# Placing q/k transposes, last keys' transposes and the first gelus in a fused top-k attention and MLP kernel

## The chip, the cores and the metric

One core of a Trainium2 chip runs the whole kernel. The metric is the device time of one execution in microseconds (us); it is 1713.43 us for the kernel before (median of three runs, 1713.32 to 1719.77).

Five engines work side by side, each through its own queue of instructions in the order in which the program wrote them: PE (TensorE, matrix products and transposes), ACT (ScalarE, activations and copies out of PSUM), DVE (VectorE), POOL (GpSimd) and SP (SyncE, which here only issues transfers). PE's results land in PSUM, a small memory; a PSUM buffer can be written again only after some engine has copied it out.

## The reference

Attention in which every query keeps its 32 largest scores, followed by an MLP with an exact gelu. There are 8 batches, 8 heads, 576 tokens and a head size of 64; the MLP takes 4608 tokens of 512 channels through 2048 hidden ones.

```python
scores = scale * np.matmul(q, k.transpose(0, 1, 3, 2))
kth = np.partition(scores, -top_k, axis=-1)[..., -top_k:-top_k + 1]
scores = np.where(scores >= kth, scores, -1000000000.0)
attn = np.exp(scores - np.max(scores, axis=-1, keepdims=True))
attn = attn / (np.sum(attn, axis=-1, keepdims=True) + 1e-09)
attn_out = np.matmul(attn, v)
x = attn_out.transpose(0, 2, 1, 3).reshape(B * S, H * D)
h = x @ w_in
g = 0.5 * h * (1.0 + erf(h * inv_sqrt2))
out = g @ w_out
```

## The kernel before

**Items and slots.** Two heads form a pair; a batch has four. An item is a tile of 128 queries of both heads of a pair. A batch has 18 items: 16 of full tiles, and two in which the last 64 queries of two pairs share a tile. Even batches have those two last, odd batches first, so the order repeats every two batches, 36 items. One loop (line 609) runs over slots n, and every slot works on several items at once:

- `scores(n + 2)`: on PE a product for the last 64 keys (`t_ps`, line 290, or 304 for the shared tiles) and one for the other 512 (`s_ps`, 294 or 315); two scaling copies on ACT. I call it S.
- `attend(n - 3)`: for every second item the product of attention and values (`o`, line 458, or 468), and an ACT copy into `xT` (463). I call it O, or the product. When the last pair of a row of tiles is through, `n_tok` grows: 256 more tokens have all four pairs' channels.
- `softmax(n - 1, e)` for both heads: a Prelu (380) and an Exp (381) on ACT, which also sums (`den`).
- `transposes(n - 2)`: three groups. First the tails, that is the last 64 keys (`tp_t`, 409 or 414), then the 512 others of each head (`tp`, 427; M below), four transposes each. Each group ends in an ACT copy to `pt` or `ptt` (410, 419, 434).
- `top_k(n)` on DVE: eight MAX8 and six MATCH_REPLACE8. The reciprocal `rden` of item n - 1 (367) stands behind its last MAX8.
- `threshold(n)` and `normalise(n - 1)` on POOL (356, 359, 392). The transposes of an item need its normalised rows.

**q and k.** Before a pair's scores can start, its q and k blocks are transposed: ten PE transposes (line 249) in three groups of 4, 2 and 4, each with one ACT copy to `qk` (253). The first group holds four key blocks, the second the tails of q and k, the third the four query blocks. `prep_at` names one slot for each pair, and all three groups fall into it: the first behind the first half of the softmax, the others behind the last M groups.

**The MLP** is cut into 1152 pieces in a fixed order (`pieces`): a block of eight first-layer pieces (`h_ps`, line 506), then a block of eight second-layer pieces (`y_ps`, 542) of the block before, and so on. As the trace counts them, most first-layer pieces are four matmuls over 256 columns of xT, a second-layer piece two over 512 columns. `behind(work, x, us)` puts the gelus of two units (517, ACT) directly behind piece x. A first-layer piece may be placed only when `ready` has reached its tokens; `mlp(n)` places up to n pieces, `left` being what the slot may still take, 7 or 8. The first layer's PSUM tag "l1" and the second layer's "l2" have two buffers each. Gelu and Exp need different tables: where ACT goes from one to the other, an ACT_TABLE_LOAD of 1.28 us shows.

**The weights** come in as 16 units in slots 1 to 16: two or three ACT operations (183, 184, 188), one or two on POOL (199, 202) and one on DVE (210) for each. They stop after slot 16.

**PSUM.** `t_ps`, `o`, `tp_t`, `tp` and `tp_qk` share one tag, "tp", with two buffers that are taken in turn. So each of these groups has to wait until the group two places before it has been copied out by ACT; and ACT takes its copies in the order in which the loop wrote them, between the softmax and the gelus.

The order within a slot is that of the loop body below. `late` says whether the second half of the softmax stands behind the first M group or ahead of the transposes.

Of the kernel before, what the change touches and what calls it, by code (L numbers as in the profile page):

```python
# [14 lines left out]
def kernel(  # L15
# [20 lines left out]
    f32, i32, u32 = mybir.dt.float32, mybir.dt.int32, mybir.dt.uint32  # L36
# [4 lines left out]
    B, H, S, D = q.shape  # L41
    P = 128
# [3 lines left out]
    NP = H // 2  # L46
    NM = S // P
    SM = NM * P
# [12 lines left out]
    work = ctx.enter_context(tc.tile_pool(name="work", bufs=2))  # L61
# [19 lines left out]
    n_pairs = B * NP  # L81
    sources = {"q": q, "k": k, "v": v}

    def raw_of(n, pair):
        return raws[n][pair % len(raws[n])]

    def load(n, pair, queue=None):
        if pair >= n_pairs:
            return
        queue = queue or nc.sync  # L90
        b, h0 = pair // NP, 2 * (pair % NP)
        t, src = raw_of(n, pair), sources[n]
        for e in range(2):
            queue.dma_start(
                out=t[:, 0:NM, e, :], in_=src[b, h0 + e, 0:SM].rearrange("(t p) d -> p t d", p=P)
            )
            queue.dma_start(out=t[e * TL : (e + 1) * TL, NM, e, :], in_=src[b, h0 + e, SM:S])
# [23 lines left out]
    START = 2 * NP + 2  # L121
# [4 lines left out]
    def unit_in(n):  # L126
        return ORDER[n - FIRST] if 0 <= n - FIRST < UNITS else None
# [66 lines left out]
    def weights_add(u):  # L194
        if u in words:
            w, _, dst = parts(u)
            d = dst.bitcast(i32)
            if on_pool(u):
                nc.gpsimd.tensor_scalar(
                    w.bitcast(i32), w.bitcast(u32), 2.0**-13, None, op0=ALU.mult  # L200
                )
            nc.gpsimd.tensor_tensor(d, d, w.bitcast(i32), op=ALU.add)
# [14 lines left out]
    items, starts = [], []  # L217
# [17 lines left out]
    KT = SM + 2 * P  # L235
    qk_of = {}

    def transpose_qk(pair, first=False):

        t = work.tile([P, KT + SM], f32, tag="qk", bufs=NP + 2, name="qk")  # L240
        qk_of[pair] = t
        rq, rk = raw_of("q", pair), raw_of("k", pair)
        blocks = [(rq, j) for j in range(NJ)] + [(rk, NM)] + [(rk, j) for j in range(NM)]

        def piece(c, n):
            tp = ps.tile([P, 512], f32, tag="tp", name="tp_qk")
            for x in range(n):
                r, j = blocks[c + x]
                nc.tensor.transpose(  # L249
                    tp[:, x * P : (x + 1) * P], r[:, j].rearrange("p e d -> p (e d)"), ident  # L250
                )
            copy = nc.vector.tensor_copy if first and c > 0 else nc.scalar.copy
            copy(out=t[:, c * P : (c + n) * P], in_=tp[:, 0 : n * P])  # L253
            if c == 0:
                load("q", pair + 2)
                load("k", pair + 2)

        return [lambda c=c, n=n: piece(c, n) for c, n in ((6, 4), (4, 2), (0, 4))]
# [17 lines left out]
    def halves(t, e, step):  # L276

        return spread(t[:, e * TL :], step + (TL if e == 0 else -TL), TL)
# [84 lines left out]
    def inverse(i):  # L363
        if i < 0 or i >= N:
            return
        st = stat_of[i]
        nc.vector.reciprocal(st["rden"], st["den"])  # L367

    def add_small(i):
        if i < 0 or i >= N:  # L370
            return
        st = stat_of[i]
        nc.gpsimd.tensor_scalar(st["den"], st["den"], 1e-9, None, op0=ALU.add)  # L373

    def softmax(i, e):

        if i < 0 or i >= N:
            return
        st, s = stat_of[i], row(i, e)
        nc.scalar.activation(s, s, func=AF.Prelu, bias=st["neg"][:, e, 1:2], scale=1.0, alpha=STEEP)  # L380
        nc.scalar.activation(  # L381
            s, s, func=AF.Exp, bias=st["bias"][:, e : e + 1], scale=1.0,
            accum_out=st["den"][:, e : e + 1],
        )
# [13 lines left out]
    def transposes(i):  # L398

        if i < 0 or i >= N:  # L400
            return []
        t, s = items[i][1], S_of.pop(i)

        def tails():
            tp = ps.tile([P, 512], f32, tag="tp", name="tp_t")
            if t < NM:
                if t % 2 == 0:
                    pt_now[0] = work.tile([P, 2 * NM + 1, 2 * P], f32, tag="pt", name="pt")
                nc.tensor.transpose(tp[:, 0:P], s[:, SM : S + TL], ident)  # L409
                nc.scalar.copy(out=pt_now[0][:, 2 * NM, t % 2 * P : (t % 2 + 1) * P], in_=tp[:, 0:P])  # L410
            else:
                pt_now[0] = ptt
                for r in range(2):
                    nc.tensor.transpose(
                        tp[0:TL, r * P : (r + 1) * P], s[:, r * S + SM : (r + 1) * S], ident
                    )
                for e in range(2):
                    c = slice(e * TL, (e + 1) * TL)
                    nc.scalar.copy(
                        out=halves(ptt[c, 0, NM, :], e, NJ * P), in_=halves(tp[0:TL, 0 : 2 * P], e, P)  # L420
                    )

        def main(e):
            tp = ps.tile([P, 512], f32, tag="tp", name="tp")
            first = e * (S + TL if t < NM else S)
            for j in range(NM):
                nc.tensor.transpose(  # L427
                    tp[:, j * P : (j + 1) * P], s[:, first + j * P : first + (j + 1) * P], ident
                )
            if t < NM:  # L430
                dst = pt_now[0][:, e * NM : (e + 1) * NM, t % 2 * P : (t % 2 + 1) * P]
            else:
                dst = ptt[:, e, 0:NM, :]
            nc.scalar.copy(out=dst, in_=tp.rearrange("p (j n) -> p j n", j=NM))  # L434

        return [tails] + [lambda e=e: main(e) for e in range(2)]

    n_tok, read = [0], [0]
# [74 lines left out]
    def gelus(us):  # L513
        for u in us:
            _, n, _, nf = units[u]
            g_of[u] = work.tile([P, nf, n], f32, tag="g", bufs=4, name="g")
            nc.scalar.activation(g_of[u], h_of.pop(u), func=AF.Gelu)  # L517
# [37 lines left out]
    pieces = []  # L555
    GELU_AT = 5

    def block(u, first):

        do, need = (l1_piece, units[u][0] + units[u][1]) if first else (l2_piece, 0)  # L560
        return [(need, lambda w=w, x=x: do(w, x)) for w in (u, u + 1) for x in range(4)]

    def behind(work, x, us):
        need, f = work[x]
        work[x] = need, lambda: (f(), gelus(us))
        return work

    pieces += block(0, True) + behind(block(2, True), 0, (0, 1))
    for u in range(2, NU, 2):
        pieces += behind(block(u - 2, False), GELU_AT, (u, u + 1))  # L570
        if u + 2 < NU:
# [2 lines left out]
    done = [0]  # L574

    def mlp(n):
        for _ in range(n):
            if done[0] >= len(pieces) or pieces[done[0]][0] > ready[0] or left[0] == 0:
                return
            pieces[done[0]][1]()  # L580
            done[0] += 1
            left[0] -= 1


    ready, left = [0], [0]
# [13 lines left out]
            scores(0)  # L599
            scores(1)  # L600

    prep_at = {}
    for b in range(B):

        for p, at in enumerate((-6, -3, 0, 2) if b % 2 == 0 else (-6, -4, -3, -2)):
            if b or p > 1:
                prep_at[starts[b] + at] = b * NP + p
    ahead = N + 4
    for n in range(ahead):

        left[0] = 7 if n < START + 2 * NP else 8
        weights_add(unit_in(n))
        scores(n + 2)
        product = attend(n - 3)
        late = n > START
        mlp(1)
        prep = transpose_qk(prep_at[n]) if n in prep_at else []
        softmax(n - 1, 0)
        for piece in prep[0:1]:
            piece()  # L620
        mlp(1)
        if not late:
            softmax(n - 1, 1)
        mlp(1)
        tr = transposes(n - 2)
        for piece in tr[:2]:
            piece()
            ready[0] = n_tok[0]
            mlp(1)
        ready[0] = n_tok[0]  # L630
        if late:
            softmax(n - 1, 1)
        add_small(n - 1)
        for piece in tr[2:] + prep[1:]:
            piece()
            mlp(1)
        mlp(left[0])
        if n < N:
            top_k(n, {3: lambda: inverse(n - 1)})
        else:  # L640
            inverse(n - 1)
        threshold(n)
        normalise(n - 1)

        weights_sign(unit_in(n))
        weights_size(unit_in(n + 1))
        if n >= FIRST:
            load_weights(n + 2)
        if n <= NP:
            load("v", n)  # L650
# [36 lines left out]
```

## Time and profile before

| | |
|---|---|
| median time | 1713.43 us |
| span of the profiled execution | 1713.1 us |
| L506 first layer on PE | 559.3 us, 2560 matmuls |
| L542 second layer on PE | 546.1 us, 1152 matmuls |
| L341 and L344, top-k on DVE | 612.5 + 202.4 and 425.4 + 212.4 us |
| L380 and L381, softmax on ACT | 223.8 and 223.3 us |
| L392, normalise on POOL | 493.6 us |
| L427, M groups on PE | 179.6 us, 1152 transposes |

A span is cut in the page into 40 slices of 43 us, with the busy share of each engine in tenths. A row of waits says which engine stood at which line, for which engine and line it waited, how long in total, how often, and the longest. A wait for a buffer is shown with the copy that freed it as the releaser. PEld is PE's loading of the stationary operand, which runs beside the matmuls where nothing holds it. Slots are not marked in the trace. I find them by the first `t_ps` after a pause: slot 30 begins at 354.61 us, slot 46 at 534.98, slot 138 at 1564.40. The last slots end near 1640 us, and PE then works through the 56 pieces that are left.

### The profile page before, as it was taken

The numbers are of one execution on the slowest core, as the hardware profiler recorded it, in microseconds if no ns is written. First come the engines' busy times: TensorE is split into PE (matmuls) and PEld (weight loads), VectorE is DVE, ScalarE is ACT, GpSimd is POOL, SyncE is SP. The second block draws the span as 40 slices with busy tenths as digits, with TensorE's granted clock in tenths as the row PEclk, the third lists the DMA queues.
The fourth block names the chain that finished last, engine by engine and source line by source line (L and its number), as shares of the span: only waits on it lengthen the run. The fifth ranks groups of instructions, "written<-read, shape, count | busy, mean of one in ns | idle before, by whom it ended". The sixth has DMA issues, their size and how long they took to land.

```text
span 1713.1 us, 24404 instructions
## 1 busy us (share of the span) xinstructions
PE 1612.4 (94%) x8480; PEld 1093.2 (64%) x8480; DVE 1428.2 (83%) x3042; ACT 1189.2 (69%) x2147; POOL 663.0 (39%) x764
## 2 busy tenths in 40 slices
PE   5558999999999999999999999999999999999999
PEld 3336567766666667666666667676666666766665
DVE  6998989988799887998889888898889987899900
ACT  5877876767676767776767776776777776777730
POOL 3667833333233332333333323333333333333310
PEclk8669999999999999999999999999999999999999
DMA  5422210011100111002100011001110010000000
GB/s 157 133 99 87 84 48 1 13 27 24 40 13 1 41 29 41 1 13 49 28 27 1 27 42 41 1 14 27 29 48 1 13 29 15 21 1 13 7 13 13
DMA packets 126715, 56.10 MB, mean 33 GB/s; under 512 B 117888, under 2 KB 117888, under 8 KB 126592
## 3 DMA queue, kind: packets, MB, share of 16 engines
q1 hardware_dynamic: 125056, 52.16, 11.4%
q0 software_dynamic: 320, 2.10, 0.3%
q8 instruction: 67, 1.10, 0.3%
q14 instruction: 56, 0.46, 0.1%
q10 hardware_dynamic: 1216, 0.30, 0.1%
HBM read 45.08 MB, written 9.44 MB: 32 GB/s over the span
## 4 chain that ended last, share of the span: by engine, by line
PE 83%; ACT 6%; POOL 0%; issue 0%; ACTq 0%; POOLq 0%
PE h_ps L506 27%; PE y_ps L542 27%; PE o L458 8%; PE s_ps L294 7%; PE tp L427 6%; PE o L468 2%; PE t_ps L290 1%; PE tp_qk L249 1%; ACT s L381 1%; ACT L381 1%; ACT s L380 1%; PE s_ps L315 1%; PE tp_t L409 1%; ACT L517 1%; ACT g L517 1%; ACT pt L434 0%
## 5 line engine op out<-in xcount | busy, mean ns | idle before, releaser
L341 DVE MAX8 top<-rest 128x8 f32<-128x576 f32 x864 | 612.5, 754 | 0.0
L506 PE MATMUL h_ps<-xT,w_in_sb 128*128 128x256 f32 (+1 forms) x2560 | 559.3, 363 | 4.3 <-ACT g L517 4.3
L542 PE MATMUL y_ps<-w_out_sb,g 128*128 128x512 f32 x1152 | 546.1, 598 | 0.0
L392 POOL TENSOR_SCALAR s<-s,rden 128x576 f32<-128x576 f32 x288 | 493.6, 1723 | 0.8 <-issue 0.4
L506 PEld LDWEIGHTS h_ps<-xT,w_in_sb 128*128 128x128 f32 x2560 | 430.3, 192 | 66.6 <-issue 15.8
L344 DVE MATCH_REPLACE8 rest<-top,rest 128x576 f32<-128x576 f32 x576 | 425.4, 750 | 0.0
L373 POOL TENSOR_SCALAR den<-den 128x2 f32<-128x2 f32 x144 | 32.0, 222 | 884.0 <-ACT s L381 883.4
L542 PEld LDWEIGHTS y_ps<-w_out_sb,g 128*128 128x128 f32 x1152 | 196.2, 190 | 173.2 <-issue 172.7
L298 ACT ACTIVATE s<-s_ps 128x1024 f32<-128x1024 f32 x128 | 131.6, 1028 | 189.7 <-PE s_ps L294 189.7
L381 ACT ACTIVATE s<-s,bias 128x576 f32<-128x576 f32 x288 | 223.3, 775 | 12.8
L380 ACT ACTIVATE s<-s,neg 128x576 f32<-128x576 f32 x288 | 223.8, 777 | 1.6 <-POOL neg L356 1.1
L434 ACT COPY pt<-tp 128x512 f32<-128x512 f32 x256 | 147.3, 576 | 109.2 <-PE tp L427 108.5
L427 PEld LDWEIGHTS tp<-ident,s 128*128 128x128 f32 x1152 | 147.0, 145 | 118.5 <-issue 57.6
L344 DVE MATCH_REPLACE8 rest<-top,s 128x576 f32<-128x576 f32 x288 | 212.4, 748 | 0.0
L341 DVE MAX8 top<-s 128x8 f32<-128x576 f32 x288 | 202.4, 747 | 5.1 <-ACT s L299 5.1
L427 PE MATMUL tp<-ident,s 128*128 128x128 f32 x1152 | 179.6, 281 | 28.3 <-ACT qk L253 13.7
L367 DVE RECIPROCAL rden<-den 128x2 f32<-128x2 f32 x144 | 23.7, 164 | 194.2 <-POOL den L373 194.2
L294 PE MATMUL s_ps<-qk 64*128 64x256 f32 x1024 | 154.5, 423 | 3.5 <-ACT s L298 3.5
L458 PE MATMUL o<-pt,raw_v 128*64 128x256 f32 x1280 | 153.6, 387 | 2.1 <-ACT pt L434 2.1
L458 PEld LDWEIGHTS o<-pt,raw_v 128*64 128x64 f32 x1280 | 86.8, 138 | 66.9 <-issue 17.9
L294 PEld LDWEIGHTS s_ps<-qk 64*128 64x128 f32 x1024 | 92.9, 196 | 27.1 <-ACT s L298 4.0
L517 ACT ACTIVATE g<-h_ps 128x512 f32<-128x512 f32 x144 | 78.6, 595 | 37.8 <-PE h_ps L506 37.1
(65 smaller groups left out, 1106.6 us busy)
## 6 DMA issues: line engine op xcount, KB each, us to landing
raw_q<-in_q_dram SPq DMA_DIRECT2D x64, 128.0 KB, 2.3
raw_v<-in_v_dram SPq DMA_DIRECT2D x64, 128.0 KB, 2.4
out_dram<-y SPq DMA_DIRECT2D x32, 256.0 KB, 2.2
raw_k<-in_k_dram SPq DMA_DIRECT2D x62, 128.0 KB, 2.4
w_out_sb<-in_moe_w_in_dram SPq DMA_DIRECT2D x12, 511.8 KB, 4.7
w_out_sb<-in_moe_w_out_dram SPq DMA_DIRECT2D x10, 511.8 KB, 4.0
w_out_sb<-in_moe_w_in_dram POOLq DMA_DIRECT2D x4, 511.8 KB, 8.6
words<-in_moe_w_out_dram SPq DMA_DIRECT2D x4, 511.8 KB, 5.0
```

The source lines that it names most:

```text
L294: nc.tensor.matmul(s_ps[:, e, c * 256 : (c + 1) * 256], lhsT=lhsT[rows, :], rhs=qk[rows, KT + c * 256 : KT + (c + 1) * 256], start=True, s ...
L298: nc.scalar.activation(spread(s, S + TL, SM), s_ps, func=AF.Copy, scale=scale)
L341: nc.vector.max(st["top"][:, e, 8 * r : 8 * r + 8], cur[e])
L344: nc.vector.match_replace(rest[:, e], st["top"][:, e, 8 * r : 8 * r + 8], cur[e], LOWEST)
L380: nc.scalar.activation(s, s, func=AF.Prelu, bias=st["neg"][:, e, 1:2], scale=1.0, alpha=STEEP)
L381: nc.scalar.activation(s, s, func=AF.Exp, bias=st["bias"][:, e : e + 1], scale=1.0, accum_out=st["den"][:, e : e + 1],)
L392: nc.gpsimd.tensor_scalar(s, s, st["rden"][:, e : e + 1], None, op0=ALU.mult)
L427: nc.tensor.transpose(tp[:, j * P : (j + 1) * P], s[:, first + j * P : first + (j + 1) * P], ident)
L434: nc.scalar.copy(out=dst, in_=tp.rearrange("p (j n) -> p j n", j=NM))
L458: nc.tensor.matmul(o[e * D : (e + 1) * D, 0:n], lhsT=vt[:, j, e, :], rhs=pt[:, e * NM + j if j < NM else 2 * NM, :], start=(j == 0), stop= ...
L506: nc.tensor.matmul(h_tile(u)[:, i, :], lhsT=w_in_sb[:, ko, f * P : (f + 1) * P], rhs=xT[:, ko, c0 : c0 + n], start=(ko == 0), stop=(ko == ...
L542: nc.tensor.matmul(y_of[sub], lhsT=g_of[u][:, i, sub * P : (sub + 1) * P], rhs=w_out_sb[:, f, :], start=(f == 0), stop=(f == FT - 1),)
```

## The change

Three things move; no arithmetic is added or removed.

1. q and k: instead of all three groups in one slot, one group a slot, behind the slot's own last transposes. A table by batch parity and pair says which slots (`slots_of`, with `first` for pairs 2 and 3). The `qk` tile is taken when the first group is placed.
2. Last keys: in slots where a product has been placed and the next MLP piece needs its tokens, the tails' transposes come directly behind the product, ahead of the softmax, and `ready` is raised then. MLP pieces can so be placed from the slot's first half on.
3. First gelus: they move from behind the first piece of the second block to behind the last piece of the first block, and slot 10 may take 8 pieces instead of 7, so that this last piece falls in slot 10. `late` begins one slot later.

```diff
     def transpose_qk(pair, first=False):
-        t = work.tile([P, KT + SM], f32, tag="qk", bufs=NP + 2, name="qk")
-        qk_of[pair] = t
         ...
         def piece(c, n):
+            if pair not in qk_of:
+                qk_of[pair] = work.tile([P, KT + SM], f32, tag="qk", bufs=NP + 2, name="qk")
+            t = qk_of[pair]
             ...
-    pieces += block(0, True) + behind(block(2, True), 0, (0, 1))
+    pieces += behind(block(0, True), 7, (0, 1)) + block(2, True)
     ...
-        for p, at in enumerate((-6, -3, 0, 2) if b % 2 == 0 else (-6, -4, -3, -2)):
-            if b or p > 1:
-                prep_at[starts[b] + at] = b * NP + p
+    slots_of = [
+        [(-8, -7, -6), (-5, -4, -3), (-2, -1, 0), (1, 2, 3)],
+        [(-10, -9, -8), (-7, -6, -5), (-4, -4, -3), (-3, -2, -2)],
+    ]
+    first = {2: (0, 1, 1), 3: (2, 2, 3)}
+    prep_in = {}
+    for pair in range(2, n_pairs):
+        b, p = divmod(pair, NP)
+        for at, piece in zip(first.get(pair, slots_of[b % 2][p]), transpose_qk(pair)):
+            prep_in.setdefault(starts[b] + at, []).append(piece)
     ...
-        left[0] = 7 if n < START + 2 * NP else 8
+        left[0] = 7 if START < n < START + 2 * NP else 8
         weights_add(unit_in(n))
         scores(n + 2)
         product = attend(n - 3)
-        late = n > START
+        late = n > START + 1
         mlp(1)
-        prep = transpose_qk(prep_at[n]) if n in prep_at else []
+        tr = transposes(n - 2)
+        if product and done[0] < len(pieces) and pieces[done[0]][0] > ready[0]:
+            for piece in tr[:1]:
+                piece()
+            tr, ready[0] = tr[1:], n_tok[0]
         softmax(n - 1, 0)
-        for piece in prep[0:1]:
-            piece()
         mlp(1)
         if not late:
             softmax(n - 1, 1)
         mlp(1)
-        tr = transposes(n - 2)
-        for piece in tr[:2]:
+        for piece in tr[:-1]:
             piece()
             ready[0] = n_tok[0]
             mlp(1)
         ...
-        for piece in tr[2:] + prep[1:]:
+        for piece in tr[-1:] + prep_in.pop(n, []):
             piece()
             mlp(1)
```

More of the change, by code (lines that the diff above doesn't have):

```diff
@@ L600 @@
             scores(1)
-    prep_at = {}
-    for b in range(B):
-        for p, at in enumerate((-6, -3, 0, 2) if b % 2 == 0 else (-6, -4, -3, -2)):
-            if b or p > 1:
-                prep_at[starts[b] + at] = b * NP + p
+    slots_of = [
[8 more added lines that the diff above has]
+            prep_in.setdefault(starts[b] + at, []).append(piece)
     ahead = N + 4
     for n in range(ahead):
-        left[0] = 7 if n < START + 2 * NP else 8
+        left[0] = 7 if START < n < START + 2 * NP else 8
         weights_add(unit_in(n))
```

## The prediction

> **What bounds the kernel now.** I first read the busy shares and the slices.
>
> ```profile
> PE 1612.4 (94%) x8480; PEld 1093.2 (64%) x8480; DVE 1428.2 (83%) x3042; ACT 1189.2 (69%) x2147; POOL 663.0 (39%) x764
> PE   5558999999999999999999999999999999999999
> DVE  6998989988799887998889888898889987899900
> PEclk8669999999999999999999999999999999999999
> ```
>
> Two stages. Up to about 150 us DVE is full and PE is half idle at a low clock; from the fifth slice on PE is at 9. There the time is the length of PE's queue: its work plus its waits. So I asked for PE's waits between 240 and 1640 us, and DVE's between 40 and 240.
>
> ```profile
> PE tp L427 <- ACT qk L253: 12.8, 6, 2.1
> PE tp L427 <- ACT pt L410: 4.5, 4, 1.1
> PE tp L427 <- ACT ptt L419: 3.9, 3, 1.3
> PE t_ps L304 <- ACT qk L253: 2.5, 3, 0.8
> PE t_ps L290 <- ACT qk L253: 2.5, 3, 0.8
> DVE rden L367 <- POOL den L373: 14.1, 5, 8.3
> ```
>
> The first five are all of PE's waits there: 26.2 us, every one for an ACT copy that has not freed a "tp" buffer. They are few and regular, so I cut the trace at the first t_ps of each slot (columns: stretch, length, busy time of PE, PEld, DVE, ACT, POOL, clock, DMA).
>
> ```profile
> 354.61:369.86 15.25, 13.12 (x82) 10.16 (x81) 13.30 (x30) 9.83 (x19) 7.21 (x7) 1.00 0.05 11
> 390.89:402.34 11.45, 10.60 (x46) 5.63 (x45) 11.45 (x26) 8.71 (x17) 5.66 (x7) 1.00 0.05 12
> 414.13:423.47 9.34, 9.34 (x36) 4.87 (x35) 9.34 (x22) 6.61 (x12) 3.56 (x6) 1.00 0.01 2
> 423.47:436.26 12.79, 12.79 (x83) 10.21 (x81) 10.82 (x24) 9.83 (x19) 5.21 (x6) 1.00 0.10 23
> 471.89:483.58 11.69, 11.69 (x72) 9.26 (x71) 9.82 (x22) 9.35 (x18) 4.07 (x6) 1.00 0.13 46
> 534.98:547.97 12.99, 11.86 (x73) 9.17 (x72) 12.30 (x27) 8.38 (x16) 6.69 (x7) 1.00 0.01 1
> 626.17:639.41 13.24, 11.94 (x74) 9.27 (x73) 11.84 (x27) 8.73 (x17) 6.09 (x7) 1.00 0.01 1
> 849.98:865.26 15.28, 13.15 (x82) 10.16 (x81) 13.07 (x30) 9.82 (x19) 6.84 (x7) 1.00 0.18 40
> 1161.69:1564.40 402.71, 394.32 (x2121) 268.32 (x2120) 352.11 (x757) 288.74 (x530) 145.90 (x181) 1.00 0.08 21
> ```
>
> In order these are slots 30, 33, 35, 36, 40, 46, 54, 74 and the period of slots 102 to 137. A plain odd slot is 9.34 us and a plain even one, with its product, 11.69: PE full in both. Slot 36 adds ten q/k transposes in three groups and no wait: 12.79 - 11.69 = 1.10 us, 0.11 a transpose, so a group of four is 0.43 of stream. A slot above these sums holds waits.
>
> **What the Trainium skill says.** "PSUM — Partial Sum Buffer", Engine vs sequencer instructions: ScalarE's queue is strict FIFO and matmuls start in program order. The trace agrees: in slot 46 a tails copy whose transposes ended by 539.0 comes out at 542.0, behind a Prelu, a table load and an Exp, and PE stands 1.13 us. "Perfetto Trace Analysis", Optimization Strategy: a gap that repeats on the engine that should be full can mean too few buffers; here these are the two of tag "tp". "ScalarE: Activation LUTs", What ACT_TABLE_LOAD costs: about 1283 ns for the load and 1380 for a drain. The trace has 1.28 for the load (353.59 to 354.87) and no drain (the gelu starts at 354.88); I use 1.28.
>
> **Part 1: tails directly behind the product.** Where the next MLP piece needs the product (slots 4, 6, 8, 10, then 18, 30, 38, 46, 54 and their repeats, from my walk through the loop), PE now has S, O, tails, piece, piece, M instead of S, O, (q/k,) tails, piece, M, piece, M. ACT gets the tails copy ahead of the first softmax half instead of behind it. No instruction is added. In slot 46's clock: the product ends and tails start at 538.66, xT's copy is 538.81 to 539.18, the tails copy would follow to about 539.5. The first piece reads channels 0 to 255, which older copies filled, so it runs at once (before, too, at 538.83); the second, at about 539.7, finds xT copied. The first M takes the buffer that xT's copy freed, the second the one that the tails copy freed. So no wait is left. Behind the tails copy on ACT stands the softmax, 0.4 us later than now; den, rden and top_k wait for it, and in this slot DVE already waits 0.69 us. DVE's own work is 9.8 us a slot (9.82 in the row of slot 40) against a mean of 10.5 on PE, which hides it.
> Gain by slot, against 11.69 (and 1.08 of stream where ten transposes are in it): slot 30 15.25 - 12.77 = 2.48; slot 38, read at slot 74, 2.51; slot 46 1.30; slot 54 1.55. Part of the first two belongs to moving the q/k group that stands ahead of the tails.
>
> **Part 2: q/k groups one a slot, last in the slot.** The same ten transposes a pair, 1.08 us of stream, now in slots -8 to +3 around a batch. Gone: slot 33's wait, 11.45 - 9.34 - 1.08 = 1.03. Slot 51 keeps its wait (two groups behind a gelu). So the gain per period of 36 slots is 2.48 + 2.51 + 1.30 + 1.55 + 1.03 = 8.9; three periods 26.6, and slot 138 another 1.3: **27.9 us**.
> Two new waits. In odd slots the group stands behind the gelus on ACT. By the clock of slots 43 and 44 the gelus end at 515.30, so a four-block copy (0.58) runs to 515.8, and the next product, which takes that buffer and stood at 515.33, now 0.43 later at 515.76. I have no row of that pair. Bounds: 0, as above, and 0.58, the whole copy. I take 0.15, for a release and a weight load that cannot run ahead: eight such slots a period (29, 31, 33, 35, 37, 45, 47, 49), three periods: +3.6. Second, in slot 39 (third slot of an even batch) the last group of the fourth pair ends behind the gelus, and slot 40's t_ps reads it at once: PE is there at 513.95 + 0.43 = 514.4, the copy is done at 515.8. That is 1.46, at most 2.0 with a restart; I take 1.5, three times: +4.5. In even slots no gelu is ahead and the copy is out before the next use: nothing.
>
> **Part 3: first gelus in slot 10.** Before, slot 11 has them behind its first piece, the pieces of the next unit stand 3.81 us for the buffers (141.19), ACT's second softmax half comes last (to 150.84), and DVE stands from 142.9 to 151.18, the 8.3 above. After: slot 10 has one piece more (0.86) and a group (0.43), so its last h ends near 134.9 + 1.3 = 136.2; gelu out at 136.9; the two weight operations 2.3 (131.24 to 133.56 before), scores copies 1.3, Prelu, table load and Exp 3.0, second half 1.8 lead to 145.3, rden at 145.9. DVE waits 3.0: 5.3 less. PE in slot 11 stands for its last M until the tails copy at 145.6 and ends the slot near 148.4, not 150.2: 1.8 less. In slots 12 to 17 ACT is the tight one (58.45 of 69.51 us) and has three gelu pairs before and after, but q/k copies for 26 instead of 40 transposes: 4.0 against 6.1 us. Slot 18 comes between 1.8 + 2.1 = 3.9 and 5.3 + 2.1 = 7.4 earlier; I take **5**, since both engines feed it. That a slot-10 softmax now stands behind tails which wait for POOL costs nothing by the same sum: in slots 4 to 9 two slots of ACT's queue are about 21 us, DVE's 21.8 (top_k 9.65, sign 1.36), little room.
> The 56 pieces behind the last slot and their PE time stay.
>
> Sum: 1713.4 - 27.9 + 3.6 + 4.5 - 5 = 1688.6.
>
> **The rivals.**
> - Waits change place. If each group behind a gelu costs a whole copy (24 times 0.58 = 13.9), slot 40 costs 2.0 (6.0) and the start brings nothing: 1713.4 - 27.9 + 19.9 = 1705. For it: buffers stay two, and 2.5 us of waits behind the same gelus are in the trace. Against: they come where t_ps, not the later product, takes the buffer.
> - All of it lands: no wait behind gelus, 9 us at the start (the whole 8.3 and more): 1713.4 - 27.9 + 4.5 - 9 = 1681. The sum of ACT's queue in slot 11 speaks against.
> - Slower. The softmax behind the tails copy empties DVE: 3.9 us of softmax in each of slots 4, 6, 8 and 10 is 15.6, and every group behind a gelu holds t_ps as in slot 40, 24 times 1.46 = 35: 1713.4 + 15.6 + 35 + 4.5 - 27.9 - 5 = 1736. For it: ACT's 21 against 21.8. Against: t_ps takes another buffer in all but that slot.
>
> **How the numbers follow.** Chances: my sum 0.65, all of it 0.15, waits in other places 0.14, slower 0.06. Range 1678 to 1704: the low end a little under the second case, the high end nearly at the first, which stands just short of 0.5% (1704.9). Faster 0.86, same 0.08, slower 0.06. The clock matters too: "TensorE: Matmul & The Clock Gate", What's actually happening, says that an idle window halves it, and the trace has 0.50 in the idle stretches before 150 us; how often that happens at the start may move the time by 2 us or so either way.
>
> **What would show it.** The waits of tp on the tails copies and on qk gone from 240 to 1640 us; slots 46 and 54 at 12.1 and 11.7, slot 30 at 12.1; a new wait of t_ps on qk of about 1.5 us, three times, and small ones of o; DVE's longest wait near 3 us instead of 8.3; slot 18 near 215. Wrong if PE's waits keep their 26 us under other names, or if DVE waits again and again for rden after 240 us.

## The result, and the profile after

The changed kernel takes 1691.75 us (median of five runs, 1689.41 to 1693.2), the kernel before 1714.55 beside it. The ratio is 0.986, 95% interval 0.9841 to 0.9879. The sum of the prediction, 1688.6, is off by about 3 us. The two parts of that sum are not as good: the periods gained 2.5 us more than forecast, and the start, where 5 us were forecast, gained nothing. One execution further down (1715.7 us, of the kernel with the weight load first, at a mean clock of 0.953 where the others had 0.978 to 0.985) is left out of the comparisons as a slow one.

The page of the kernel after: the busy row, and the slices of PE, DVE and PE's clock.

```profile
PE 1611.4 (95%) x8480; PEld 1093.3 (65%) x8480; DVE 1428.8 (85%) x3042; ACT 1188.1 (70%) x2147; POOL 662.5 (39%) x764
...
PE   5659899999999999999999999999999999999999
...
DVE  6999798998889888998889888898889988899900
...
PEclk8669999999999999999999999999999999999999
```

The work is the same (PE 1611.4 us busy against 1612.4), the span is 23 us shorter. So waits went. These are all of PE's waits between 240 and 1640 us:

```profile
PE t_ps L291 <- ACT qk L254: 3.8, 3, 1.3
PE t_ps L305 <- ACT qk L254: 2.5, 3, 0.8
```

and this is DVE's one group of waits between 40 and 240 us:

```profile
DVE rden L368 <- POOL den L374: 13.9, 7, 7.9
```

PE's 26.2 us have become 6.3. No wait for the tails' copy is left; the three of 1.3 us are new and are those that the prediction put at slot 40; the three of 0.8 us are those of slot 51, which it left standing. DVE's row has hardly moved, 13.9 against 14.1 us, with a longest wait of 7.9 us where 3 was forecast.

The prediction also named a sign of being wrong: that DVE waits again and again for rden after 240 us. It does, but it did so before, and more. DVE's waits between 240 and 1640 us, before and after:

```profile
DVE rden L367 <- POOL den L373: 180.1, 93, 8.7
DVE rden L368 <- POOL den L374: 155.6, 87, 8.7
```

In slots 30, 46 and 54 below PE is full while DVE is not, so waits of DVE cost nothing there; as a sign they don't tell the two cases apart.

By slots (columns as before: stretch, length, busy time of PE, PEld, DVE, ACT, POOL, clock, DMA):

```profile
169.53:189.12 19.59, 14.68 (x73) 8.83 (x72) 11.74 (x23) 8.83 (x16) 10.90 (x8) 0.83 0.44 138
356.16:368.31 12.15, 12.15 (x76) 9.65 (x75) 10.84 (x26) 8.93 (x18) 5.08 (x7) 1.00 0.10 22
390.07:399.85 9.78, 9.78 (x40) 5.26 (x39) 9.78 (x24) 7.04 (x13) 3.99 (x6) 1.00 0.05 11
455.52:466.74 11.22, 9.95 (x41) 5.08 (x39) 10.66 (x25) 8.49 (x16) 4.91 (x7) 1.00 0.11 25
530.58:542.74 12.16, 12.16 (x77) 9.66 (x76) 10.84 (x26) 8.92 (x18) 5.14 (x7) 1.00 0.10 22
619.90:631.62 11.72, 11.72 (x73) 9.34 (x72) 10.26 (x24) 8.80 (x17) 4.51 (x6) 1.00 0.01 1
1147.57:1542.62 395.05, 392.92 (x2116) 268.13 (x2115) 351.66 (x757) 288.00 (x529) 145.31 (x181) 1.00 0.08 21
```

These are slots 14, 30, 33, 39, 46, 54 and the period of slots 102 to 137. Slots 30 and 46 are an even slot and one group of four (11.69 + 0.43 = 12.12), slot 54 a bare even slot, slot 33 an odd slot and a group (9.34 + 0.43 = 9.77): PE is full in all of them. Slot 39 has 1.45 us over 9.77, as the next slot's first product waits for its copy. Slot 14 is new: 19.59 us, with every engine well under its length and PE's clock down to 0.83.

Two figures carry the rest of the story. I read them at the first `s_ps` matmul of a slot: when slot 19 begins (the **start**: everything in which other engines than PE have a say), and the time from there to slot 141 (the **periods**).

| kernel | slot 19 begins, us | slots 19 to 141, us |
|---|---|---|
| before | 235.3 | 1363.4 |
| after | 236.2 | 1339.4 |

In the periods 24.0 us went. 1.7 us of them are a stretch of 3.4 us at half clock at 454 us in the trace of before (slot 38 took 16.96 us, its repeat 15.28). It comes directly behind one of the 2.1 us stands that the change removes:

```profile
453.24 0.66 PE L427 MATMUL tp<-ident,s 128*128 128x128 f32 x4 [2.12 <-ACT qk L253]
```

The forecast read slot 38 at its repeat and has no such stretch, so 22.3 us are to be held against it. The start lost 0.9 us.

How far can one trace be trusted on the start? Seven of the kernels here, the changed one and six of the experiments, are the same program up to slot 10, and DVE is full there. Yet the reciprocal that DVE runs in slot 10 comes at 131.1 us in one of these traces and at 132.7 us in another. So up to 1.6 us of a difference in the start can come from the execution and not from an edit. Where that matters I also count from this reciprocal to slot 19, which leaves that part out: 103.5 us before and 103.5 after.

### The profile page after: what moved, and what is told of

The parts are those of the page before. It is cut to its first block, busy times and chain, and to the rows that moved or that the text cites. A ratio compares the mean times of both kernels' runs of the same rounds, so it can differ in the third digit from the quotient of the medians.

```text
span 1690.0 us, 24403 instructions
## 1 busy us (share of the span) xinstructions
PE 1611.4 (95%) x8480; PEld 1093.3 (65%) x8480; DVE 1428.8 (85%) x3042; ACT 1188.1 (70%) x2147; POOL 662.5 (39%) x764
## 4 chain that ended last, share of the span: by engine, by line
PE 87%; ACT 5%; DVE 5%; POOL 1%; issue 1%; DMA 1%; SPq 0%; ACTq 0%; POOLq 0%
PE h_ps L507 29%; PE y_ps L543 28%; PE o L459 8%; PE s_ps L295 7%; PE tp L428 7%; DVE top L342 2%; PE o L469 2%; DVE rest L345 2%; PE tp_qk L250 2%; PE t_ps L291 2%; ACT s L382 1%; PE tp_t L410 1%; PE s_ps L316 1%; ACT s L381 1%; ACT L518 1%
```

## The experiments

The first question was where the 5 us of the start went. The trace shows slot 14 standing. From the timeline of the kernel after (start, duration; SPq is SyncE issuing transfers):

```profile
168.76 0.38 SPq L94 DMA_DIRECT2D raw_q<-in_q_dram  x1
...
172.75 0.51 SPq L97 DMA_DIRECT2D raw_k<-in_k_dram  x1
...
173.37 1.26 SPq L161 DMA_DIRECT2D xT<-in_moe_w_out_dram  x2
...
177.60 0.37 ACT L464 COPY xT<-o 128x256 f32<-128x256 f32 x1 [4.54 <-DMA xT<-in_moe_w_out_dram]
...
178.84 0.79 PE L507 MATMUL h_ps<-xT,w_in_sb 128*128 128x256 f32 x1 [4.91 <-DMA xT<-in_moe_w_out_dram]
```

The raw weights of unit 14 are staged in the last 512 columns of `xT` (line 159). In slot 14 the product's copy and the first layer both touch `xT`, and both wait for that transfer. It stands on SP's queue behind eight q/k loads, which the third q/k group of slot 13 issues: from 168.76 to 173.26, 4.5 us. That group is the sixth pair's (pair 5, counted from 0). Before, it stood in slot 14, and its loads came behind the weight load. From there the wait runs on: the copy is ahead of the softmax on ACT, DVE then stands 7.85 us for rden, and PE drops to half clock at 177.8 us for 6.8 us.

**Leaving out one part each.** Three kernels, each the changed one without one of its parts, and one with the q/k loads of slot 13 behind the weight load.

Without the tails order:

```diff
-        if product and done[0] < len(pieces) and pieces[done[0]][0] > ready[0]:
+        if False:
```

> The changed kernel with the last keys' transposes back behind the softmax half in every slot; q/k table and first gelus as changed. Theory, the parts add up slot by slot: slots 30, 38, 46 of each period get back the 1.3 us wait of slot 46 before and slot 54 its 1.55, three periods, and slot 138 another 1.3, so 3 x 5.45 + 1.3 = 17.7 us: about 1709 against 1691.75; PE waits for tp on the tails copy, 13 times. Rival, the tails order matters only where a q/k group stands ahead of the tails: at most 5 us, under 1697.

Measured 1709.1 us; ratio to before 0.9966 (0.9951 to 0.9981). PE's waits between 240 and 1640 us in that kernel:

```profile
PE tp L428 <- ACT pt L411: 11.2, 10, 1.1
PE tp L428 <- ACT ptt L420: 3.9, 3, 1.3
```

Thirteen waits for the tails' copy are back, ten plus three, besides the 6.3 us of the kernel after. The periods take 1357.2 us, 17.8 more than after. The first theory stands: the tails order is worth its wait in every slot where it applies.

Without the q/k table:

```diff
-        for at, piece in zip(first.get(pair, slots_of[b % 2][p]), transpose_qk(pair)):
-            prep_in.setdefault(starts[b] + at, []).append(piece)
         ...
+                prep_at[starts[b] + at] = b * NP + p
         ...
+        prep = transpose_qk(prep_at[n]) if n in prep_at else []
         softmax(n - 1, 0)
+        for piece in prep[0:1]:
+            piece()
         ...
-        for piece in tr[-1:] + prep_in.pop(n, []):
+        for piece in tr[-1:] + prep[1:]:
```

> The changed kernel with all three q/k groups of a pair back in one slot, in the places of before; tails order and first gelus as changed. Theory A (slot 14 of the changed kernel stands because the weight load into xT queues on SP behind the eight q/k loads that the group of slot 13 issues): here these loads are issued a slot earlier, slot 14 has no wait for a transfer and the start gains its 5 us, while the periods lose about 1 us of waits in slots 30, 33 and 38 each and get back 1.45 in slot 40: 1688 to 1692. Theory B (slots 12 to 17 are held by ACT's own queue, the wait for the transfer only takes the place of others): the start gains nothing, and 14 more transposes' copies make it worse: 1694 to 1698.

Measured 1686.72 us, ratio 0.9838 (0.9825 to 0.9851): about 5 us **less** than with the table, and below both ranges. Slot 19 begins at 230.9 us instead of 236.2, and the xT load is issued at 168.72, with nothing ahead of it on SP. The expectation had one detail the wrong way round: the sixth pair's eight loads are issued here a slot later, from 182.28 us on, and not earlier. The periods take 1340.6 us, only 1.2 more than with the table; PE's waits there are 6.4 us against 6.3. Part 2 of the change lost, at the start, more than it brought.

Without the first gelus in slot 10:

```diff
-    pieces += behind(block(0, True), 7, (0, 1)) + block(2, True)
+    pieces += block(0, True) + behind(block(2, True), 0, (0, 1))
         ...
-        left[0] = 7 if START < n < START + 2 * NP else 8
+        left[0] = 7 if n < START + 2 * NP else 8
         ...
-        late = n > START + 1
+        late = n > START
```

> The changed kernel with the first gelus and the slot 10 limit as before; tails order and q/k table as changed. Theory A: the gain of the gelus is lost in slot 14 at the weight load into xT, which is issued at a time that the gelus don't set, so leaving them out costs little: 1690 to 1694. Theory B: gelus in slot 10 bring their 5 us and something else of the change costs them at the start: 1696 to 1698.

Measured 1693.89 us, 0.988 (0.9867 to 0.9893). Slot 19 begins at 238.2, 1.9 us later than after. That fits the first theory's range; it doesn't yet say what the gelus are worth without slot 14's wait.

With the weight load first:

```diff
             if c == 0:
-                load("q", pair + 2)
-                load("k", pair + 2)
+                held.append(pair + 2)
+                if slot_now[0] != 13:
+                    load_held()
         ...
             load_weights(n + 2)
+        load_held()
```

> The changed kernel; in slot 13 alone the eight q/k loads are issued behind the weight load into xT instead of ahead of it. Theory A (the order on SP's queue is the cause): that load is issued near 169.6 us instead of 173.4, the wait of slot 14 on PE falls from 4.9 us to 1 or less, DVE's wait from 7.9 to 3 or 4, slot 19 begins about 4 us earlier: 1687 to 1688. Theory B (ACT's queue holds these slots): the wait goes, ACT's queue takes its place and the time stays at 1691 to 1692.

Measured 1685.11 us in five executions, 0.9828 (0.9814 to 0.9841). The load is issued at 168.11 us, ACT's copy waits 0.4 us instead of 4.5, and the list of waits of this kernel has (its lines are up to nine further down):

```profile
DVE rden L377 <- POOL den L383: 4.2, 3, 1.9
...
PE h_ps L516 <- DMA xT<-in_moe_w_out_dram: 1.8, 1, 1.8
```

These are waits between 160 and 195 us: the first row is all of DVE's (8.4 in the kernel after), the second all that PE waits for the transfer (4.9 there). Slot 19 begins at 228.7, 7.5 us earlier than after and 6.6 earlier than before. So the order on SP's queue made the wait long; the gain in time, 6.6 us, is larger than the 4 us expected. PE's wait for the transfer is still 1.8 us, where 1 or less was expected.

**Is the transfer needed there at all?** The copy of slot 14 writes columns 256 to 511 of `xT`, the transfer columns 640 to 1151. But it was issued as two transfers of two channel rows each, and from first to last word such a transfer spans the lower columns of its second row.

```diff
-            for a in range(2):
+            for a in range(4):
+                at = half.offset + (r + a // 2) * P * 4 * DM + a % 2 * 2 * WS + 1
                 queue.dma_start(
-                    out=t[:, 2 * a : 2 * a + 2].bitcast(u16),
+                    out=t[:, a].bitcast(u16),
                     ...
```

> The changed kernel; the weight load into xT in slot 13 is four transfers of one channel row each instead of two of two rows, in its old place on SP's queue behind the q/k loads. A transfer of two rows spans, from its first to its last word, columns that the product's copy and the first layer's matmuls of slot 14 use, though it writes none of them; a transfer of one row doesn't. Theory A (slot 14 stands only for this overlap of spans, and the late issue makes it long): no wait for a transfer is left in slot 14, slot 15 begins 7 us earlier than the changed kernel's 189.5, and the time is a little under that of the loads in the other order: 1683 to 1685. Theory B (the transfer itself is what slots 14 and 15 need, the weights of a later unit): the wait comes back at the weight operations of slot 14 or 15, and the time stays above 1689.

Measured 1682.78 us, 0.9803 (0.9784 to 0.9822). Its timeline:

```profile
173.71 0.51 SPq L97 DMA_DIRECT2D raw_k<-in_k_dram  x1
...
174.19 2.86 PE L505 MATMUL h_ps<-xT,w_in_sb 128*128 128x256 f32 x12
174.26 2.01 SPq L162 DMA_DIRECT2D xT<-in_moe_w_out_dram  x4
174.31 0.37 ACT L462 COPY xT<-o 128x256 f32<-128x256 f32 x1 [0.28 <-PE o L457]
```

The load is issued even later than in the kernel after, 174.26 us, and nobody waits: the first layer has begun before it. So the second theory falls. Slot 14 never needed the data; it waited for an overlap of spans. Counted from DVE's reciprocal in slot 10, slot 19 comes after 96.9 us here and after 97.1 with the weight load first, against 103.5 both before and after the change.

**The waits that the table leaves.** Two table entries changed, on top of the kernel with the weight load first:

```diff
-        [(-8, -7, -6), (-5, -4, -3), (-2, -1, 0), (1, 2, 3)],
-        [(-10, -9, -8), (-7, -6, -5), (-4, -4, -3), (-3, -2, -2)],
+        [(-8, -7, -6), (-5, -4, -3), (-2, -1, 0), (1, 2, 2)],
+        [(-10, -9, -8), (-7, -6, -5), (-4, -4, -4), (-3, -2, -2)],
```

> The kernel with the q/k loads of slot 13 behind the weight load, and two entries of the q/k table changed: the fourth pair of an even batch in slots 1, 2, 2 instead of 1, 2, 3, the third pair of an odd batch in -4, -4, -4 instead of -4, -4, -3. Theory A (the two waits of t_ps on a q/k copy behind gelus, 3.8 and 2.5 us in the trace, are all that the table costs in the periods): both vanish, with no new wait of PE between 240 and 1640 us, and 6.3 us go: 1678 to 1679 against 1685.2. Theory B (three groups in one slot bring back waits for the tp buffers as before): 1682 to 1686.

Measured 1681.04 us, 0.979 (0.9771 to 0.981). Both rows of `t_ps` are gone; in their place PE waits three times 0.4 us in a slot that now has three groups. The periods take 1333.9 us instead of 1339.3: 5.4 of the 6.3 us. The time lies between the two expectations, the trace nearer to the first.

**The gelus.** Alone, on the kernel before, with the three gelu lines of the diff above as in the change:

> The kernel before with the first gelus and the slot 10 limit of the changed kernel alone; tails and q/k groups as before. Theory A (slots 12 to 17 of before have no transfer to wait for, so the gelus bring their whole 4 to 5 us): DVE's wait of 8.3 us in slot 11 falls to about 1 to 3, slot 18 begins 4 to 5 us earlier: 1709 to 1711 against 1714.5. Theory B (as leaving the gelus out of the changed kernel cost only 2 us): 1712 to 1714.

Measured 1713.16 us against 1716.26 beside it, 0.9982 (0.9971 to 0.9993). Slot 19 begins at 232.8, 2.5 us earlier than before; DVE's longest wait is 2.4 us. So the wait of 8.3 us did fall, and most of it didn't reach PE. The time lies between the two theories. The first of them took it that there is no transfer to wait for; but PE now waits 1.6 us for the one into xT, which it doesn't in the trace of before.

Left out of the kernel with one-row transfers:

> The kernel with the weight load into xT in four one-row transfers (1682.8 us), with the first gelus and the slot 10 limit as before. Theory A (the gelus' 4 to 5 us were there all along, and in the changed kernel the wait for the transfer ate part of them): without them slot 19 begins 4 to 5 us later than 229.3, 1687 to 1688. Theory B (they are worth 2 us, as by the two runs without the four transfers): 1684 to 1685.

Measured 1687.36 us, 0.983 (0.9811 to 0.9849), 4.6 us more than with the gelus, while by the traces slot 19 begins at 230.7, only 1.4 us later. Both are right for what they are: the trace with the gelus is of the slowest of its four executions (1684.6 us), the trace without them of the fastest of four (1686.0). Counted from DVE's reciprocal in slot 10, the three pairs of traces give 2.4 us (in the changed kernel), 3.2 (alone) and 2.7 (here) for the gelus. The three pairs of medians give 2.1, 3.1 and 4.6. I take it as about 3.

And the q/k table left out of that kernel:

> The kernel with the weight load into xT in four one-row transfers (1682.8 us), with all three q/k groups of a pair in one slot as before. Theory A (the q/k table cost 5 us at the start only through the transfer, and is worth 1 to 2 us in the periods next to the new tails order): slot 19 begins about where it does with the table, at 229 to 230, and the time is 1684 to 1685. Theory B (the table also slows the start by ACT's extra copies in slots 8 to 13): the start is 1 us or more earlier without it and the time stays at 1682 to 1683.

Measured 1686.86 us, 0.9832 (0.9812 to 0.9851). Slot 19 begins at 228.8, with the table at 229.3; the periods take 1340.6 against 1339.3. By these traces the table, where no one waits for the transfer, costs half a microsecond at the start and brings 1.3 in the periods. But they are again of the slowest of four executions (1684.6) and the fastest of five (1685.51). The median of 1686.86 is above both expectations. It lies 4 us above the 1682.78 with the table, and no execution of one kernel reaches those of the other. So the table brings between 1 and 4 us here; what makes the difference isn't shown.

**Together.** One-row transfers, the weight load first, and the two table entries:

> Everything together: the changed kernel with the two table entries, the q/k loads of slot 13 behind the weight load, and that load in four one-row transfers. By the sum: 1685.2 - 6.3 for the table - 1.5 for the last wait for a transfer in slot 14 = 1677.4. If DVE or ACT holds the start once the transfer is out of the way, as at 1679 or the value of the run without the four transfers.

Measured 1677.46 us (1676.36 to 1679.39), ratio to before 0.9772 (0.9752 to 0.9791). The sum that was expected is 1677.4. This beats the changed kernel by 14 us (the kernel before took 1716.26 beside it, 1714.55 beside the changed kernel).

| kernel | slot 19 begins, us | slots 19 to 141, us |
|---|---|---|
| without the tails order | 237.5 | 1357.2 |
| without the q/k table | 230.9 | 1340.6 |
| without the gelus | 238.2 | 1339.3 |
| weight load first | 228.7 | 1339.3 |
| one-row transfers | 229.3 | 1339.3 |
| weight load first, two entries | 229.3 | 1333.9 |
| gelus alone | 232.8 | 1363.3 |
| one-row transfers, without the gelus | 230.7 | 1339.3 |
| one-row transfers, without the q/k table | 228.8 | 1340.6 |
| together | 229.5 | 1333.9 |

## Why the prediction was right, and where it wasn't

**Right on what bounds the kernel.** PE's waits from 240 us on went from 26.2 to 6.3 us and the periods shrank with them. DVE, ACT and POOL had the slack that was claimed: in the period of slots 102 to 137 PE is now busy 392.92 of 395.05 us, DVE 351.66, ACT 288.00.

**Right on the tails order.** Slots 46 and 54 were forecast at 12.1 and 11.7 us and took 12.16 and 11.72. Leaving it out gave 1709.1 where 1709 was worked out from the waits.

**Right on both new waits, one too large.** Slot 40's wait for slot 39's copy was taken as 1.5 us; slot 39 is 1.45 over its sum. (The 1.46 in the prediction doesn't come out of the times beside it, 515.8 and 514.4, which are 1.4 apart.) The small waits behind gelus were taken as 0.15 each, from bounds of 0 and 0.58. No wait of `o` shows in PE's list, and the even slots after them are 0.02 to 0.08 over their sums (slot 46, 12.16 - 12.12 = 0.04). That is nearly the lower bound: the term of 3.6 us was under 2, and with it goes most of the 2.5 us that the periods gained beyond the 19.8 forecast (27.9 - 3.6 - 4.5).

**Wrong on the start.** The step that failed is the one that has slot 18 come between 3.9 and 7.4 us earlier, and takes 5. It came 1.2 us later. Slot 11 did better than forecast: it ended at 147.1 us where 148.4 was given, DVE stood 2.8 us in slots 11 and 12 where 3.0 was, and slot 14 still began 4.5 us ahead of before. Then slot 14 gave it all back. I had costed the moved q/k groups by PE's stream and ACT's copies alone, and never asked what else a group does: the third one issues eight loads. Moving the sixth pair's from slot 14 to slot 13 put 4.5 us of issuing ahead of a load on which, through a span and not through data, slot 14 hangs. With that wait gone slot 19 begins 6 to 7 us ahead of before.

**Right in sum there, but not by its terms.** With the wait gone the start gains a little more than the 5 us forecast, yet not from what the 5 us were made of. The gelus were given 1.8 to 5.3 us; they bring about 3. The table was given 2.1 us, for fewer copies on ACT in slots 12 to 17; without the transfer's wait the traces show it costing half a microsecond at the start. That term rested on ACT being the tight engine there, with 58.45 of 69.51 us. The row it was read from, that of before, shows PE and DVE fuller:

```profile
150.22:219.73 69.51, 64.12 (x359) 39.43 (x358) 64.61 (x130) 58.45 (x101) 56.85 (x40) 1.00 0.29 80
```

The tails order was held to bring nothing at the start. The trace without it has slot 19 begin 1.3 us later, 2.1 counted from DVE's reciprocal; but by the medians the whole loss, 17.35 us, is no more than the 17.8 of the periods. So 0 to 2 us, and this isn't settled. Together these terms come to some 3 to 5 us of the 6.4 and 6.6 that slot 19 gains, counted from DVE's reciprocal, in the two kernels with the wait shortened or gone; the rest isn't assigned to a part.

**The q/k table** was credited with slot 33's wait and a share in those of slots 30 and 38. Next to the tails order it is worth 1.2 us in the periods. The tails order had already removed the waits of slots 30 and 38, since without the table too no M group waits for a copy of q/k or of the tails. And slot 40's new wait, 3.8 us in all, takes back the 2.5 us that PE otherwise waits behind slot 33.

So the total was near partly by luck: two errors, of 2.5 us in the periods and about 6 at the start, had opposite signs.

## What to carry to other kernels

When a piece of work moves, list everything it issues, transfers and buffer releases included, and look at the queue of the engine that issues them: a load ahead of another in that queue delays it as surely as an instruction would. When an instruction waits for a transfer, check that the words really overlap; splitting the transfer so that its spans don't may remove the wait. And add up the start and the steady part apart, since a total that fits can hide two that don't. Last, a trace is one execution: before a microsecond is read from two traces, see where each lies among the executions of its kernel.

## What the runs showed of the hardware

Issuing a q/k load took SyncE 0.4 to 0.6 us, so that eight of them held its queue for 4.5 us (168.76 to 173.26), while each landed 2.1 to 2.4 us after its issue, in the medians of the list of transfers. During a stand of 4.9 us PE's clock went to half (at 177.8 us) and stayed there for 6.8 us. The stands of 1.3 us in the periods were not followed by any half clock. Stands of 2.1 us come six times in the periods of before and six times in those of the gelus alone; one in each was followed by 3.4 us at half clock, from 454.0 and from 359.5 us on.
